# A fused attention and two-layer mixture kernel: attention units in pairs, the w_out decode on 1024 columns, and a new order of steps

## The chip, the cores and the metric

One core of a Trainium2 chip runs the whole program. The metric is the device time of one execution in microseconds (us): median of three runs. Engines are TensorE (PE, matmuls), VectorE (DVE), ScalarE (ACT), GpSimd (POOL) and SyncE (SP). Here SP issues every transfer between DRAM and on-chip memory, in one queue of instructions. "SBUF" is the on-chip memory and "PSUM" the accumulators that PE writes.

## The reference, cut to what matters

Three blocks follow each other: windowed attention, a layer with SoLU and a norm, and a mixture of four experts.

```python
scores = scale * q @ k^T                       # 2 batches, 8 heads, 576 positions, 64 wide
masks  = plain window of 32 (heads 0-3), window 32*4 with step 4 (heads 4-7)
attn   = exp(scores - max); attn /= sum + 1e-9
x      = attn @ v                              # -> 1152 tokens x 512

h      = x @ w_in                              # 512 -> 1024
solu   = h * softmax(h)
ln     = (solu - mean) / sqrt(var + 1e-6) * g_ln
x      = ln @ w_out                            # 1024 -> 512

p      = domain_probs / (sum + 1e-9)           # 4 experts
out    = sum over e of p[:, e] * (relu(x @ w1[e]) @ w2[e])
```

## The kernel before, in words

**Precision.** A product of two fp32 operands is made of three matmuls on a high and a low part (hi·hi, hi·lo, lo·hi). So each operand is split before use: a cast writes the high part (`xhi`, `wh`, `hh`), a subtraction writes the low part (`xlo`, `wl`, `hl`). The attention weights `w_in` and `w_out` arrive as 64-bit numbers and are decoded by `convert` (two ACT passes, two DVE passes and one DVE or POOL pass) ahead of the split.

**Attention.** There are twelve units: for each batch, three of the plain heads (P, t = 0 to 2, 192 positions each) and three of the dilated heads (D, t = 0 to 2). A unit is the generator `att_U`, a chain of steps: scores on PE (L275, after two matmuls that write the mask, L266), maximum (L296, DVE), subtraction (L298, DVE), exponential (L301, ACT), sum (L303, DVE), reciprocal (L305, DVE), scaling into the tile `pd` (L307, POOL or DVE), transposition (PE, L326, with a copy out of PSUM, `pt`; for the five units in `ASWAP` a DVE transposition, L312, and a trip through DRAM, `da` and back), the product with v on PE (L337), and the split into `xhi` and `xlo` (L250).

**First layer.** `H.t` (t = 0 to 8) multiplies 128 tokens by `w_in` (L367: 24 matmuls of 512 columns, in four groups by the quarter of `w_in` that they need) and applies SoLU: maximum `nmx` (L372), exponential (L374), product with the sum (L376), shift (L379 or L381). `T.t` transposes the result and splits it into `hh` and `hl`. T.0 to T.2 go through PE (L398). T.3 to T.8 go through a DVE transposition (L414, L412) and through DRAM: `dt` is written, `et` is loaded, then `hh` (L174 or L176) and `hl` (L436) are made of `et`. The two `et` tiles alternate: T.3, T.5 and T.7 use `et1`, T.4, T.6 and T.8 use `et0`. `X.c.dp` multiplies a chunk c of three tiles (384 tokens) by half of `w_out` (L449, 48 matmuls of 384 columns). Chunk 0 and chunk 1 share one pair of tiles `hh`, `hl`: what T.3 to T.5 write there must wait until X.0 has read it.

**Mixture.** `up` (L562) and `down` (L634) run over eight halves of experts, with seven products for eight in `up`.

**What sets the order.** The program is written step by step by the string `ORDER`: each word advances one generator by one step, and a `+` takes the other engine where a step has two to choose from (POOL for DVE, DVE for ACT). So `ORDER` fixes the order of instructions on each engine. `F.n` stands for n matmuls that compute nothing and keep PE busy (L86). `lP`, `lD`, `lI`, `lO`, `lvp` and `lvd` are the loads. PE writes into two pools of PSUM, `psm` (H, X) and `psa` (attention, transpositions), two tiles each.

Of the kernel before, what the change touches and what calls it, by code (L numbers as in the profile page):

```python
# [27 lines left out]
EXPB = ()  # L28
ASWAP = ("UD.0.1", "UD.1.1", "UD.2.1", "UP.1.1", "UP.2.1")

ORDER = """
F.3 lP.0.0+ UP.0.0 lI.4 VI.4+ lD.0.0 VI.4 F.1 UP.0.0+ UP.0.0 lD.1.0+ VI.4 F.1 lP.1.0+ UD.0.0 UD.1.0 UP.0.0 VI.4 lI.0 UP.0.0+ VI.4 VI.0 lP.2.0 UD.0.0 UD.0.0+
UD.0.0+ UP.1.0 UP.0.0+ VI.4+ UP.0.0+ UD.1.0 UD.1.0+ UP.1.0 F.10 lD.2.0+ UP.2.0 UD.1.0+ VI.0 UD.0.0 VI.0+ VI.0 UP.1.0+ UD.1.0 UP.1.0+ VI.4+ lI.1+ UD.1.0+ VI.0+
UD.2.0+ UD.1.0+ lI.2+ F.3 UD.0.0 UD.0.0+ VI.0 UP.1.0+ UP.2.0 lvp.0.0+ VI.1+ VI.1+ UP.1.0+ UP.2.0+ VI.0 lvd.1.0+ F.1 UP.0.0 UD.2.0 UD.2.0 UP.2.0 UP.0.0 F.4
UD.1.0 UD.0.0 F.3 VI.1+ UD.1.0 VI.2+ UP.0.0 VI.2 UD.0.0 UP.2.0+ UP.1.0+ VI.1 UP.0.0 VI.1 VI.1 VI.2 UP.0.0+ lI.3 UD.1.0+ VI.2+ UP.1.0 lvp.1.0 UD.1.0 H.0+ lvd.0.0
UP.1.0 VI.3 UP.2.0+ UD.1.0+ UP.1.0 UD.2.0 UD.0.0+ VI.1 VI.3+ VI.2 VI.3 UP.1.0 UP.1.0 lD.1.1+ UD.0.0 lO.0.0+ H.0+ UD.1.1 VI.3 VI.2 UD.2.0+ lO.0.1 misc+ UD.1.1
H.1 UD.2.0 lD.0.1+ lvd.2.0+ UP.2.0+ UD.1.1+ UD.0.0 VO.0.1 VI.2+ lvp.0.1 lP.0.1 UD.2.0 lvd.2.1 H.1 VO.0.1+ UD.2.0 UD.2.0 UD.0.1 VI.3 VO.0.1+ UD.1.1 UP.0.1 UD.0.1
VI.3 lD.2.1 lvp.2.0+ lP.2.1 UD.1.1 UP.0.1 H.0 UD.0.1+ UD.0.1 UP.0.1+ UD.0.1+ UD.0.1+ UD.2.0 VO.0.1+ VI.3+ VO.0.0 UD.2.1 VO.0.0 lP.1.1+ VO.0.1+ H.0 lO.1.1+
VO.0.0 UD.2.1+ UD.2.0 UP.0.1+ UD.2.0 UD.0.1+ H.0+ H.1 H.0+ UD.0.1+ UD.0.1 UD.2.1 VO.0.0 H.1 H.0 UD.0.1+ UD.1.1 endE+ VO.0.0+ UD.2.1+ UP.2.0 UP.2.0 UD.1.1+
UP.2.1+ lvd.0.1+ VO.0.1+ lvd.1.1 UP.2.1+ UP.0.1 UD.2.1+ UP.2.0 UP.0.1 UP.2.0 VO.1.1+ VO.0.1+ VO.1.1 H.2 H.2+ H.1+ UP.2.1+ H.0+ UP.0.1+ UD.1.1+ VO.0.0+ UP.0.1  # L40
VO.1.1+ UP.2.0 VO.0.0+ H.1+ T.0 UP.2.1 UP.0.1 T.0+ UD.1.1 UD.2.1+ lO.1.0+ H.1+ T.0 UP.0.1 VO.1.1+ VO.1.1+ H.3+ UP.2.1 lO.2.1+ H.2+ T.0+ VO.1.0+ UP.0.1 UP.0.1+
VO.1.0 UD.1.1 VO.1.1+ UP.2.1+ UP.1.1+ UD.0.1 VO.1.0+ UP.1.1+ VO.1.0 H.2+ VO.1.0+ UP.1.1 UP.2.1+ UD.0.1+ UD.0.1+ H.3+ UD.2.1+ UD.1.1 H.2 H.1+ VO.1.0 UP.1.1+ T.1+
H.3+ lO.2.0+ UD.2.1+ H.2+ UD.1.1 H.3 UD.1.1 UD.2.1+ VO.2.1+ UP.1.1 VO.1.0+ H.4+ VO.2.0 VO.1.1 UP.2.1 VO.2.0 T.1+ T.2 T.1 H.3+ UP.1.1 UP.1.1+ VO.2.0+ H.4 H.5+
lvp.1.1+ UD.2.1+ H.5+ VO.2.1+ UP.2.1 H.4 T.2 VO.2.1+ VO.2.0+ VO.2.1+ lvp.2.1+ UP.2.1 VO.2.0+ lO.3.0 VO.2.1+ H.4 T.2 VO.2.1+ UP.1.1+ T.1+ T.2 lO.3.1 UP.2.1 H.3+
VO.2.0+ H.5+ UP.1.1+ VO.3.0 UP.2.1+ VO.2.0 H.5+ VO.2.1+ UP.2.1+ UP.1.1+ H.5+ VO.3.1 VO.3.0+ UD.2.1+ VO.3.1 VO.3.0 UD.2.1 X.0.1+ X.0.0 VO.3.1+ UP.1.1+ VO.3.0+
VO.3.1 VO.3.0+ VO.3.0 VO.3.1 endA T.3+ VO.3.1 VO.3.1 T.3+ UP.1.1 VO.3.0+ H.4+ T.3+ X.0.1+ T.4 X.0.0+ H.5 X.0.0 UP.1.1 T.4+ X.0.1+ T.4 T.3+ T.5+ UD.2.1 H.6+ T.3
H.8 T.3+ T.5+ H.6+ T.5 H.6 H.6+ T.4+ H.6 T.5+ H.7+ T.6 T.4 H.8 H.8 T.5 T.4 H.8+ T.5+ H.8+ H.7 X.1.0 T.6 T.6 T.6 T.8+ H.7 T.8+ H.7 T.6+ T.8+ T.6 H.7+ T.8+ X.1.0+
T.7+ T.8+ X.1.1 X.1.1+ T.7+ T.8 T.7+ sc T.7 endH T.7+ T.7 X.1.0 XQ.0 X.1.1 X.2.0 XQ.0 XQ.0 lW.0 WP.0+ WP.0 X.2.1+ XQ.0 WP.0 WP.0 WP.0 XQ.0 XQ.0 XQ.0+ WP.0 u.0+
WP.0 endX WP.0 X.2.0+ XQ.1 WP.0+ WP.0 WP.0 XQ.0+ lV.0+ WP.0 X.2.1 XQ.0+ XQ.0+ XQ.0 WP.0+ XQ.0+ XQ.0 XQ.0 WP.0 lW.1 XQ.0+ WP.0+ u.0 u.0+ XQ.1 XQ.1 WP.0 XQ.0 u.0
u.0 WP.0 WV.0 XQ.1 u.0+ WV.0 u.0 XQ.1 u.0 u.0 XQ.1+ u.1+ u.0 WP.0 u.0+ XQ.1 u.0 XQ.1+ u.0+ u.0 u.1 u.0 u.0 u.0 XQ.1 u.0+ u.0 u.0+ WV.0 WV.0 u.1+ u.0+ WP.1+ u.0  # L50
WP.1 u.1 u.1+ XQ.1+ u.0+ lW.2 u.0+ u.1 XQ.1 WP.1 lV.1 u.1 u.1 d.0 u.1+ u.1 XQ.1+ XQ.1 d.1+ u.1+ XQ.1 u.1+ WP.1 WP.1 d.0+ d.1 d.3+ WP.1+ u.1+ WP.1 XQ.1 u.1+
WP.1+ u.1 WP.1 XQ.1+ u.1+ WP.1 d.3 d.2 u.1 WP.1 d.2 u.1 WP.1 u.1 u.1+ WP.1+ u.1 WP.1+ WP.1+ u.1 u.1+ WP.1 u.1 WP.1 WP.1+
# [3 lines left out]
def fused_kernel(ctx, tc, qkp, qkd, vp, vd, w_in, w_out, gp, w1, w2, out):  # L56
# [61 lines left out]
    pds = [ap1.tile([128, 3, 128], F32, name=f"pd{i}", tag=f"pd{i}") for i in range(3)]  # L118
    sms = [ap1.tile([128, 6, 65], F32, name=f"sm{i}", tag=f"sm{i}") for i in range(3)]
    identb = ap1.tile([128, 128], BF16, name="identb", tag="identb")  # L120
    nc.vector.tensor_copy(identb, ident)
    for sm in sms:
        nc.vector.memset(sm[:, :, 64:65], 1e-9)
# [42 lines left out]
    def pick():  # L166
        return nc.gpsimd if alt[0] != late[0] else nc.vector
# [59 lines left out]
    def load_out(j, t):  # L227
        nc.sync.dma_start(out=cvr[:, 1024 * t:1024 * t + 1024].bitcast(I64), in_=w_out[256 * j + 128 * t:256 * j + 128 * t + 128, :])

    def conv_out(j, t):  # L230
        sl = slice(512 * t, 512 * t + 512)
        a = cva[:, sl]
        yield from convert(cvr[:, 1024 * t:1024 * t + 1024], a)
# [572 lines left out]
```

## Time and profile before

| what | us |
|---|---|
| median of three runs (527.78, 528.5, 528.66) | 528.5 |
| the profiled execution, its time | 528.32 |
| its span, first to last instruction | 526.5 |
| PE busy in the span | 513.6 (98%) |
| DVE busy | 356.4 (68%) |
| ACT, POOL busy | 190.6, 186.7 |

Some 1.8 us of the profiled execution's time lie outside the span. An engine's busy time is the time in which at least one of its instructions runs; PE at 98% has 12.9 us without work in the whole span.

### The profile page before, as it was taken

To read this page: it belongs to the slowest core of one execution; us is meant where nothing else is said; L and a number is where in the kernel's file an instruction comes from. 1 tells how busy PE (TensorE), PEld (TensorE's weight loads), DVE (VectorE), ACT (ScalarE), POOL (GpSimd) and SP (SyncE) were. 2 spreads that over 40 slices of the span, in tenths; PEclk is the share of its full clock that TensorE was granted. 3 is DMA by queue.
4 is the path that set the end of the run, shared out by engine and by line. 5 is a ranking of instruction groups with operands and counts; after the bars stand their busy time and mean duration, and the time that the engine had idled before them with its cause. 6 is when DMAs were issued, how large, how long until landed. Compare 5 with 4: busy or idle time off the path is not lost.

```text
span 526.5 us, 9419 instructions
## 1 busy us (share of the span) xinstructions
PE 513.6 (98%) x3971; PEld 457.9 (87%) x3971; DVE 356.4 (68%) x474; ACT 190.6 (36%) x294; POOL 186.7 (35%) x131
## 2 busy tenths in 40 slices
PE   7789999998999999999999999999999999999997
PEld 3568889888999999998989899898989989898986
DVE  7999898484999875754775485568448655853532
ACT  3766884363153422421422233142223213312200
POOL 3334321111345632830661273047117313820300
PEclk9999999999999999999999999999999999999999
DMA  8984462546062001300400040040005002000022
GB/s 321 409 319 149 146 202 78 143 159 200 1 225 95 1 1 50 111 1 1 159 1 1 8 153 0 2 153 7 2 0 161 1 0 81 0 1 1 1 81 100
DMA packets 24490, 46.44 MB, mean 88 GB/s; under 512 B 4480, under 2 KB 9088, under 8 KB 24064
## 3 DMA queue, kind: packets, MB, share of 16 engines
q1 hardware_dynamic: 24448, 45.84, 25.4%
q8 instruction: 31, 0.51, 0.4%
q14 instruction: 11, 0.09, 0.1%
HBM read 39.34 MB, written 6.49 MB: 87 GB/s over the span
## 4 chain that ended last, share of the span: by engine, by line
PE 90%; DMA 4%; DVE 2%; ACT 1%; issue 1%; SPq 1%; ACTq 0%
PE pa L634 19%; PE pm L634 18%; PE pm L562 17%; PE pa L562 17%; PE pm L367 9%; PE pm L449 6%; DMA draw<-in_moe_w_in_dram 2%; PE pa L337 1%; DMA dt<-st 1%; DMA et<-dt 1%; PE pa L275 1%; PE pa L398 1%; SPq L151 0%; DVE hl L436 0%; ACT eva L192 0%
## 5 line engine op out<-in xcount | busy, mean ns | idle before, releaser
L575 DVE SCALAR_TENSOR_TENSOR hl<-ct,hh 128x512 fp32r<-128x512 f32 (+1 forms) x64 | 64.1, 1018 | 32.4 <-ACT hh L573 32.4
L573 ACT ACTIVATE hh<-ct 128x512 fp32r<-128x512 f32 (+1 forms) x64 | 42.2, 682 | 50.8 <-DVE ct L605 21.3
L634 PE MATMUL pa<-wl,hh 128*128 128x512 f32 (+1 forms) x148 | 57.3, 387 | 0.0
L634 PE MATMUL pa<-wh,hh 128*128 128x512 f32 (+1 forms) x148 | 57.2, 387 | 0.0
L634 PE MATMUL pa<-wh,hl 128*128 128x512 f32 (+1 forms) x148 | 57.1, 386 | 0.0
L562 PE MATMUL pm<-xoh,hl 128*128 128x256 f32 (+1 forms) x192 | 56.8, 296 | 0.0
L562 PE MATMUL pa<-xoh,hl 128*128 128x256 f32 (+1 forms) x192 | 56.8, 296 | 0.0
L562 PE MATMUL pm<-xol,hh 128*128 128x256 f32 (+1 forms) x192 | 56.8, 296 | 0.0
L562 PE MATMUL pa<-xol,hh 128*128 128x256 f32 (+1 forms) x192 | 56.8, 296 | 0.0
L562 PE MATMUL pm<-xoh,hh 128*128 128x256 f32 (+1 forms) x192 | 56.8, 296 | 0.0
L562 PE MATMUL pa<-xoh,hh 128*128 128x256 f32 (+1 forms) x192 | 56.8, 296 | 0.0
L634 PE MATMUL pm<-wl,hh 128*128 128x512 f32 (+1 forms) x144 | 55.7, 387 | 0.0
L634 PE MATMUL pm<-wh,hh 128*128 128x512 f32 (+1 forms) x144 | 55.7, 387 | 0.0
L634 PE MATMUL pm<-wh,hl 128*128 128x512 f32 (+1 forms) x144 | 55.6, 386 | 0.0
L481 POOL TENSOR_TENSOR wl<-wl,wh 128x1024 fp32r<-128x1024 f32 x7 | 16.9, 2413 | 94.7 <-ACT wh L176 94.7
L639 DVE SCALAR_TENSOR_TENSOR xf<-pm,pr,xf 128x512 f32<-128x512 f32 (+1 forms) x32 | 23.6, 738 | 31.1 <-PE pm L634 31.1
L639 DVE SCALAR_TENSOR_TENSOR xf<-pa,pr,xf 128x512 f32<-128x512 f32 (+1 forms) x32 | 23.6, 738 | 30.3 <-PE pa L634 30.3
L589 POOL TENSOR_TENSOR ct<-ct,ct 128x512 f32<-128x512 f32 (+1 forms) x16 | 24.1, 1506 | 54.3 <-ACT ct L587 54.3
L176 ACT CAST wh<-wl 128x1024 fp32r<-128x1024 f32 x16 | 16.8, 1052 | 70.3 <-PE pa L634 39.8
L481 POOL TENSOR_TENSOR hl<-sw,hh 128x512 fp32r<-128x512 f32 x20 | 29.4, 1475 | 28.2 <-ACT hh L176 28.2
L562 PEld LDWEIGHTS pm<-xoh,hh 128*128 128x128 f32 x192 | 36.4, 190 | 0.3
L562 PEld LDWEIGHTS pm<-xol,hh 128*128 128x128 f32 x192 | 36.4, 190 | 0.3
(200 smaller groups left out, 1258.5 us busy)
## 6 DMA issues: line engine op xcount, KB each, us to landing
wl<-in_moe_w_dram SPq DMA_DIRECT2D x16, 512.0 KB, 4.3
cvr<-in_moe_w_out_dram SPq DMA_DIRECT2D x8, 512.0 KB, 3.5
rw<-in_moe_w_dram SPq DMA_DIRECT2D x8, 512.0 KB, 4.9
wh<-in_moe_w_dram SPq DMA_DIRECT2D x8, 512.0 KB, 6.5
draw<-in_moe_w_in_dram SPq DMA_DIRECT2D x3, 1024.0 KB, 11.9
qkD<-in_qkd_dram SPq DMA_DIRECT2D x6, 448.0 KB, 9.9
dt<-st SPq DMA_DIRECT2D x5, 512.0 KB, 3.0
et<-dt SPq DMA_DIRECT2D x10, 256.0 KB, 4.8
```

Of the source, the lines that this page charges most:

```text
L176: nc.scalar.copy(out, in_)
L275: nc.tensor.matmul(ps[32 * g:32 * g + 32, j, 64 * m:64 * m + 64], lhsT=qt[rows, h, xq:xq + 32], rhs=kt[rows, h, xq:xq + 64], start=False, ...
L337: nc.tensor.matmul(po[64 * (g % 2):64 * (g % 2) + 64, j, o:o + 32], lhsT=vt[rows, m, g, :], rhs=pt[rows, m, g, :], start=True, stop=True)
L367: nc.tensor.matmul(pm[:, n, :], lhsT=xx[:, kk, cols], rhs=ww["in", kk][:, 512 * n:512 * n + 512], start=(n_ == 0 and i < 2), stop=(n_ == K ...
L449: nc.tensor.matmul(pm[:, dd, 0:CW], lhsT=w_, rhs=x_[:, f, :], start=(f == 0 and i == 0), stop=(f == KF - 1 and i == 2))
L481: pick().tensor_tensor(out=out, in0=a, in1=b, op=op)
L562: nc.tensor.matmul(ps[:, ff, 0:n], lhsT=a[:, kk, fc], rhs=b[:, kk, :], start=kk == 0 and m == 0, stop=kk == 1 and m == 2)
L573: nc.scalar.activation(out=hv, in_=src, func=AF.Relu)
L575: nc.vector.scalar_tensor_tensor(out=lv, in0=src, scalar=0.0, in1=hv.bitcast(F32), op0=ALU.max, op1=ALU.subtract)
L589: poolv().tensor_tensor(out=c12, in0=c21, in1=c22, op=ALU.add)
L634: nc.tensor.matmul(po[:, 0, 0:dn], lhsT=h_[:, f, cols], rhs=w_, start=(f == 0 and i == 0), stop=(f == 3 and i == 2))
L639: nc.vector.scalar_tensor_tensor(out=acc[:, t, dc], in0=po[:, 0, 0:dn], scalar=pr[:, t, e:e + 1], in1=acc[:, t, dc], op0=ALU.mult, op1=ALU ...
```

## The change

The units of attention run in pairs: two units share one chain of steps, and each DVE, ACT or POOL step of the chain works on both at once, 768 elements per partition for 384. Seven chains replace twelve: in batch 0 P0 alone, D0+D1, P1 alone and P2+D2; in batch 1 P0+P1, D0+D1 and P2+D2. The matmuls are those of before. The scaling (now L304) writes in place, so the `pd` tiles go, and two `sm` tiles stand for three. Two pairs (four units) go through DRAM for the transposition, where five units did; so PE makes 24 transpositions of attention weights for 21. `conv_out` decodes `w_out` in four steps of 1024 columns for eight of 512 (its loads stay eight). The string `ORDER` is new from end to end. The core of the diff:

```diff
-EXPB = ()
-ASWAP = ("UD.0.1", "UD.1.1", "UD.2.1", "UP.1.1", "UP.2.1")
+PB = 2
+PAIRS = (((("P", 0),), (("D", 0), ("D", 1)), (("P", 1),), (("P", 2), ("D", 2))), ((("P", 0), ("P", 1)), (("D", 0), ("D", 1)), (("P", 2), ("D", 2))))
+ASWAP = ((1, 1), (2, 1))
 ORDER = """
-F.3 lP.0.0+ UP.0.0 lI.4 VI.4+ lD.0.0 VI.4 F.1 UP.0.0+ UP.0.0 lD.1.0+ VI.4 F.1 lP.1.0+ UD.0.0 UD.1.0 UP.0.0 VI.4 lI.0 UP.0.0+ VI.4 VI.0 lP.2.0 UD.0.0 UD.0.0+
+lD.0.0 lP.0.0+ F.10 lD.1.0+ U.0.0 lP.1.0+ U.0.0+ U.1.0 U.0.0 U.1.0 lP.2.0 U.0.0 lI.0 F.3 U.0.0+ U.0.0+ U.1.0 U.2.0 U.0.0+ F.1 U.1.0+ F.3 U.0.0 U.2.0 U.2.0+
...
-    def conv_out(j, t):
-        sl = slice(512 * t, 512 * t + 512)
-        a = cva[:, sl]
-        yield from convert(cvr[:, 1024 * t:1024 * t + 1024], a)
...
+    def conv_out(j):
+        yield from convert(cvr, cva)
...
+        for t in range(2):
+            sl = slice(512 * t, 512 * t + 512)
+            hi, lo = whi["out", j][:, sl], wlo["out", j][:, sl]
...
-        pick().tensor_tensor(out=pd.rearrange("p m (j x) -> p j m x", j=2), in0=sm.rearrange("p (j m) x -> p j m x", j=2),
-                             in1=st[:, 3].rearrange("p (j m) -> p j m", j=2).unsqueeze(3).to_broadcast([128, 2, 3, 64]), op=ALU.mult)
+        pick().tensor_tensor(out=sm, in0=sm, in1=st[:, 2].rearrange("p (c j) -> p c j", j=2).unsqueeze(3).to_broadcast([128, nc_, 2, 64]), op=ALU.mult)
```

Three places show what the order moves.

The first is SP's queue, the first loads of the program. The order before (`draw_196`, `draw_358`, `draw_390`, `draw_480` are pieces of `w_in`; the last three are its second, third and fourth quarter):

```order
1 L151 DMA qkP_110<-in_qkp_dram 128x832
2 L209 DMA draw_196<-in_moe_w_in_dram 128x512
3 L151 DMA qkD_113<-in_qkd_dram 128x896
4 L151 DMA qkD_114<-in_qkd_dram 128x896
5 L151 DMA qkP_111<-in_qkp_dram 128x832
6 L212 DMA draw_196<-in_moe_w_in_dram 128x512
7 L151 DMA qkP_112<-in_qkp_dram 128x832
8 L151 DMA qkD_115<-in_qkd_dram 128x896
9 L212 DMA draw_358<-in_moe_w_in_dram 128x1024
10 L212 DMA draw_390<-in_moe_w_in_dram 128x1024
11 L159 DMA vp<-in_vp_dram 128x768
12 L154 DMA vd_117<-in_vd_dram 128x768
13 L212 DMA draw_480<-in_moe_w_in_dram 128x1024
```

And with the change (`draw_505` is the fourth quarter):

```order
1 L147 DMA qkD_113<-in_qkd_dram 128x896
2 L147 DMA qkP_110<-in_qkp_dram 128x832
3 L147 DMA qkD_114<-in_qkd_dram 128x896
4 L147 DMA qkP_111<-in_qkp_dram 128x832
5 L147 DMA qkP_112<-in_qkp_dram 128x832
6 L208 DMA draw_260<-in_moe_w_in_dram 128x512
7 L147 DMA qkD_115<-in_qkd_dram 128x896
8 L205 DMA draw_260<-in_moe_w_in_dram 128x512
9 L208 DMA draw_377<-in_moe_w_in_dram 128x1024
13 L208 DMA draw_411<-in_moe_w_in_dram 128x1024
14 L147 DMA qkP_119<-in_qkp_dram 128x832
16 L208 DMA draw_505<-in_moe_w_in_dram 128x1024
```

The queries and keys of batch 0 now stand ahead of `w_in`, and two loads of batch 1 (`qkP_119`, `qkP_120`) ahead of its last quarter.

The second is DVE, the first steps of the softmax. Before (`st` is a small tile, `sm` the scores, one number per unit):

```order
12 L296 TENSOR_REDUCE st<-pa 128x6
13 L298 TENSOR_TENSOR sm_131<-pa,st 128x6x64
14 L194 TENSOR_SCALAR cva<-cva 128x512
15 L196 SCALAR_TENSOR_TENSOR cva<-draw_196,cva 128x512
16 L303 TENSOR_REDUCE st<-sm_131 128x6
17 L198 ISA cva<-draw_196,cva 128x1024
18 L296 TENSOR_REDUCE st<-pa 128x6
19 L298 TENSOR_TENSOR sm_132<-pa,st 128x6x64
```

With the change:

```order
11 L292 TENSOR_REDUCE st<-pa 128x6
12 L294 TENSOR_TENSOR sm_128<-pa,st 128x2x3x64
13 L300 TENSOR_REDUCE st<-sm_128 128x6
14 L302 RECIPROCAL st<-st 128x6
15 L292 TENSOR_REDUCE st<-pa 128x12
16 L294 TENSOR_TENSOR sm_129<-pa,st 128x2x6x64
17 L292 TENSOR_REDUCE st<-pa 128x6
18 L294 TENSOR_TENSOR sm_128<-pa,st 128x2x3x64
19 L300 TENSOR_REDUCE st<-sm_129 128x12
```

The pair D0+D1 is one row of twelve maxima where two rows of six stood, and the decode of `w_in` (L194 to L198) no longer stands between the first softmax steps.

The third is DVE around the transpositions T.3 to T.8. Before (the number behind `et` or `st` tells tiles apart: `et_1582` is T.4's, `et_1656` T.6's; `hh` and `hl` of T.3 and T.5 are made by ACT and POOL there):

```order
141 L414 STREAM_TRANSPOSE st_1615<-e 128x8x4x32
142 L372 TENSOR_REDUCE nmx<-pm 128x1
143 L436 TENSOR_TENSOR hl<-et_1582,hh 128x8x128
144 L376 SCALAR_TENSOR_TENSOR e,nsum<-e,pm 128x1024
145 L372 TENSOR_REDUCE nmx<-pm 128x1
146 L414 STREAM_TRANSPOSE st_1659<-e 128x8x4x32
147 L376 SCALAR_TENSOR_TENSOR e,nsum<-e,pm 128x1024
148 L174 CAST hh<-et_1656 128x8x128
149 L436 TENSOR_TENSOR hl<-et_1656,hh 128x8x128
```

With the change (`et_1320` is T.3's, `et_1411` T.4's, `et_1504` T.5's and `et_1600` T.7's):

```order
114 L417 STREAM_TRANSPOSE st_1409<-e 128x8x4x32
115 L236 SCALAR_TENSOR_TENSOR wl_1415<-cva,gp_sb,wh_1414 128x512 x2
116 L170 CAST hh<-et_1320 128x8x128
117 L441 TENSOR_TENSOR hl<-et_1320,hh 128x8x128
118 L170 CAST hh<-et_1411 128x8x128
119 L419 STREAM_TRANSPOSE st_1506<-e 128x8x4x32
120 L170 CAST hh<-et_1504 128x8x128
121 L441 TENSOR_TENSOR hl<-et_1504,hh 128x8x128
122 L377 TENSOR_REDUCE nmx<-pm 128x1
123 L381 SCALAR_TENSOR_TENSOR e,nsum<-e,pm 128x1024
```

All `hh` and `hl` of chunk 1 now stand in one block, and only one `nmx` (that of H.8, row 122) comes behind it. On PE this goes with H.6 and H.7 standing ahead of X.0, so that only H.8 lies between X.0 and X.1, where H.6, H.8 and H.7 did.

## Rows read from the trace of the kernel before

**Rows 1.** The page's busy times, and windows of the core (span, busy time by engine).

```profile
PE 513.6 (98%) x3971; PEld 457.9 (87%) x3971; DVE 356.4 (68%) x474; ACT 190.6 (36%) x294; POOL 186.7 (35%) x131
...
0.00:45.00 45.00, 37.41 (x832) 25.19 (x833) 39.06 (x81) 26.51 (x42) 15.95 (x24) 1.00 0.84 320
45.00:67.00 22.00, 22.00 (x375) 18.10 (x374) 20.55 (x38) 18.10 (x32) 7.43 (x7) 1.00 0.51 159
...
100.00:147.60 47.60, 45.56 (x245) 42.70 (x244) 34.75 (x47) 16.49 (x24) 11.07 (x7) 1.00 0.38 117
147.60:526.50 378.90, 375.65 (x2221) 341.83 (x2219) 236.47 (x272) 109.02 (x166) 145.09 (x89) 1.00 0.14 48
```

**Rows 2.** Waits of PE: waiting line, releaser, us in total, times, longest.

```profile
PE pa L337 <- ACT pt L176: 1.2, 1, 1.2
PE pa L326 <- ACT pt L176: 1.1, 1, 1.1
PE pa L275 <- DMA qkD<-in_qkd_dram: 1.1, 1, 1.1
...
PE pm L449 <- DVE hl L436: 0.8, 1, 0.8
...
PE pm L449 <- POOL hl L436: 0.6, 1, 0.6
PE pm L449 <- issue: 0.6, 1, 0.6
```

**Rows 3.** SP's timeline: start, length, transfer issued.

```profile
16.42 2.85 SPq L228 DMA_DIRECT2D cvr<-in_moe_w_out_dram  x2
...
24.37 0.33 SPq L159 DMA_DIRECT2D vp<-in_vp_dram  x1
...
26.59 0.33 SPq L154 DMA_DIRECT2D vd<-in_vd_dram  x1
```

**Rows 4.** PE's timeline: start, length, instruction, idle time before in brackets.

```profile
19.53 0.84 PE L326 MATMUL pa<-ident,pd 128*128 128x128 f32 x6 [1.12 <-ACT pt L176]
...
44.70 0.49 PE L326 MATMUL pa<-ident,pd 128*128 128x128 f32 x3
...
45.94 0.90 PE L337 MATMUL pa<-pt,vp 64*64 64x32 f32 x48
46.77 0.50 PE L367 MATMUL pm<-wh,xhi 128*128 128x512 f32 x1
...
95.10 0.63 PE L367 MATMUL pm<-wh,xhi 128*128 128x512 f32 x2
...
112.44 0.44 PE L449 MATMUL pm<-hl,wh 128*128 128x384 f32 x1 [0.65 <-POOL hl L436]
```

**Rows 5.** Groups of one form up to 150 us, DVE, ACT and POOL: busy us, mean ns.

```profile
L298 DVE TENSOR_TENSOR sm<-pa,st 128x384 f32<-128x384 f32 x12 | 6.5, 552 | 0.2
...
L436 DVE TENSOR_TENSOR hl<-et,hh 128x1024 fp32r<-128x1024 f32 x4 | 4.9, 1220 | 0.1
...
L174 DVE CAST hh<-et 128x1024 fp32r<-128x1024 f32 x3 | 2.1, 692 | 5.1 <-DMA et<-dt 5.1
...
L190 ACT ACTIVATE draw<-draw 128x1024 int32<-128x1024 uint32 x3 | 3.5, 1178 | 0.3 <-DMA draw<-in_moe_w_in_dram 0.3
...
L176 ACT COPY xf<-pm 128x768 f32<-128x768 f32 x4 | 3.2, 801 | 18.0 <-PE pm L449 18.0
...
L307 POOL TENSOR_TENSOR pd<-sm,st 128x384 f32<-128x384 f32 x11 | 9.4, 859 | 21.6 <-DVE st L305 20.9 <-DVE wl L225 0.7
```

**Rows 6.** The transfers through DRAM by kind (KB each, us to landing), and one of them on ACT's timeline.

```profile
et<-dt SPq DMA_DIRECT2D x1, 512.0 KB, 3.4
...
106.05 1.05 ACT L176 CAST hh<-et 128x1024 fp32r<-128x1024 f32 x1 [2.80 <-DMA et<-dt]
```

**Rows 7.** SP's timeline at the transposition T.4: the two loads of `et0`.

```profile
97.60 1.40 SPq L431 DMA_DIRECT2D et<-dt  x2
```

**Rows 8.** DVE and POOL on the timeline at 132 us.

```profile
132.25 2.31 DVE L481 TENSOR_TENSOR xol<-xf,xoh 128x1024 fp32r<-128x1024 f32 x1
...
132.07 1.39 POOL L481 TENSOR_TENSOR sw<-rw,rw 128x512 f32<-128x512 f32 x1 [4.14 <-DMA rw<-in_moe_w_dram]
```

## What the change would do to the time: the prediction

> **What bounds the kernel now.** I read the page's busy times and the windows first [rows 1]. PE works 513.6 of 526.5 us. From 147.6 us on, in the mixture, it lacks 3.3 us in 379, and there the change leaves the order of the work much as it was. Of the other 9.6 us, 7.6 lie before 45 us and 2.0 between 100 and 147.6; between 45 and 67 us PE never waits. So two places can give or take time. The waits of PE name them [rows 2]: early it waits for copies out of PSUM (1.2 and 1.1 us), for queries and keys (1.1) and for other starts; late it waits three times ahead of the product with `w_out`, 0.8, 0.6 and 0.6 us, 2.0 in all. But PE busy does not mean PE useful: early it also runs `F` matmuls that compute nothing (26 in both orders). The early stretch is therefore judged by how far the real work has come at a given time, not by idle time. The second engine is DVE [rows 1]: 39.1 of the first 45 us and 20.6 of the next 22. A lead that PE gains early must pass that stretch.
>
> **The change, part by part.**
>
> *Pairs.* A DVE step on 384 elements takes 0.55 us [rows 5], one on 1024 (of `hl`) 1.22. On the line through both, 0.55 + 384 × 0.67/640, a step on 768 takes 0.95 us (an estimate). Two steps of 0.55 become one of 0.95. With three wide DVE steps per chain and five pairs that is 15 × 0.15 = 2.3 us of DVE; ACT, POOL and the small reciprocals gain in the same way. None of this is PE time. It counts only where PE waits for a chain, and there a pair has a price: the first unit of a pair waits for the second one's scores and for the wider step, 0.4 us at each step.
>
> *The early stretch.* I walked the first instructions of each engine by hand in the new order, with the durations of rows. The anchors are landings. Counting bytes in SP's order, the 16th load of the new order (the last quarter of `w_in`) ends at the same sum, 8672 KB, as the load whose landing released SP at 26.59 us; the ninth (the second quarter) ends at 4640 KB, where SP stood at 16.42; `qkP_120` at 7648 KB, just below the 24.37 of 7840 KB, so at 23.9 [rows 3]. From there:
> - The scores of P0 come at 5.9 us (864 KB in place of 416 lie ahead). The second quarter lands at 16.4; ACT decodes it in two passes of some 1.15 us each [rows 5] and then copies `pt` of D0+D1 (0.8 us, as the copy of 768 elements of `xf`), to 19.45. The products with v begin at 19.5.
> - The scores of batch 1's plain pair wait for `qkP_120`, 23.9 to 24.85; H.0's first quarter ends at 26.2.
> - The last quarter of `w_in` lands at 26.6. ACT decodes it in two passes and copies `pt` of P1, to 29.4, then the transpositions of P2+D2 run, the scores of D0+D1 at 30.9, H.1 from 31.9. H.0's fourth group needs POOL's low part of the last quarter, ready at 39.0, and runs from 38.85 to 40.2. H.1 ends at 43.15.
>
> Before, this point (the transposition of batch 1's first plain unit after H.1) is at 44.70, and one product with v is still to come, 0.83 us (45.94 to 46.77) [rows 4]. So the new order leads by 1.55 + 0.83 = 2.4 us. The 24 transpositions for 21 come after that point: 0.84 us for six is 0.14 each with the pipeline's fill [rows 4], taken as 0.33 for three. Left: 2.05.
>
> *45 to about 95 us.* I cost this at nothing. PE does not wait here before [rows 1]. In my walk the new order has one wait, H.4's third group for the low part of the D0+D1 pair, 0.4 us. If DVE's lead is gone, every us that DVE is late is one that PE loses (rival below).
>
> *The w_out decode.* Four steps for eight save overheads of about 1.2 us on DVE and 1.5 on ACT (the same line for 1024 against two of 512). PE is ahead of neither there. Nothing, and at most that 1.2 us if DVE should set the pace.
>
> *Two tiles moved ahead of X.0.* This is the costly part. T.3, T.4 and T.5 write the pair `hh`, `hl` that X.0 reads, so none of them may be made before X.0 ends. Before, X.0 ends at 95.10 and X.1 could begin near 111.5 (112.44 less its wait of 0.65 and the first matmul) [rows 4]: H.6, H.8 and H.7 give 16.4 us, 5.46 each. Now only H.8 does. The chain to T.5 is serial, since T.5 reuses `et1` of T.3. After X.0's end: 0.04, `hh` of T.3 0.7, `hl` 1.22 [rows 5], then SP may load `et1` again, 3.4 us for this one transfer of 512 KB [rows 6], then `hh` 0.7 and `hl` 1.22. That is 7.3 us against 5.46, and X.1's second matmul needs it: PE waits about 1.7 us. Around X.0's own start I find two shorter waits: 0.35 for `hl` of T.2 and 0.65 for the PSUM tile that H.7's product with the sum must leave (DVE has the 1024-column decode in that place). X.2 gains by the move: its last input, T.8, is transposed early enough for the 96 matmuls of X.1 to hide its trip, so the waits of 0.6 and 0.8 us ahead of it go. Late waits now 0.4 + 0.35 + 0.65 + 1.7 = 3.1 us, before 2.04. Loss 1.06.
>
> *Start of the mixture.* The loads of `w1` now stand ahead of those of `w2` on SP. By the walk the first operands keep a margin of 0.4 to 1 us. Nothing; without the margin up to 1 us.
>
> **Sum.** 528.32 − 2.4 + 0.33 + 1.06 = 527.3 us, beside a median of 528.5 for the runs shown, 0.2 above the profiled one.
>
> *A rule against it.* In one row a DVE subtraction with two SBUF operands of 1024 elements took 2.31 us while POOL ran a two-input step beside it [rows 8], against 1.22 for the usual one [rows 5]. The pairs' scalings run on POOL with two SBUF inputs (one of 384 took 0.86 before [rows 5]; one of 768 now, an estimate of 1.75). The Trainium skill, GPSIMD Engine Reference, section 1, Specifications, says that GpSimd's SBUF interfaces are shared with VectorE, with contention against DVE instructions that have two SBUF inputs; by that rule the row at 132 us is no accident, and the trace agrees in that row. What it would make of this change is a rival below.
>
> **Rivals.**
> - *The late waits do not come* (523.9 to 525.5). The order puts the decode's last parts and T.5's DRAM trip where the walk is least sure: if `hl` of T.3 or the reload of `et1` is quicker, or H.7's tile frees in time, the 3.1 us of new late waits shrink to none. 528.32 − 2.4 + 0.33 − 2.04 = 524.2. For it: PE ran without a wait from 45 to 100 us before. Against it: the serial chain after X.0 is made of four rows that do not get shorter.
> - *DVE eats the lead* (528.3 to 529.4). DVE is busy 20.6 of 22 us between 45 and 67 [rows 1]. If the pairs' wider steps come late by 2 us anywhere before X.0, PE waits there and the early lead is gone: 528.32 + 0.33, less any of the late loss that the delay takes over, 528.3.
> - *Slower: the reload of `et1` takes as long as that of `et0` did* (529.6 to 531.9). The loads of `et0` for T.4 were issued from 97.60 to 99.0 [rows 7], and ACT found them landed only at 106.05 [rows 6], 7 to 8 us in place of 3.4. If the one reload behind X.0 takes 8, PE waits 4.6 us longer: 531.9. It decides from 6.0 us on (527.3 + 2.6 = 529.9). Against it: other transfers of the same kind took 4.8 us or less (median), and nothing large is queued ahead of it.
> - *Slower: POOL beside DVE* (529 to 531). Each DVE step with two SBUF inputs that meets a POOL step costs 0.5 to 1.1 us more (2.31 − 1.22 in the one row). Three to four such meetings in the stretch where DVE sets the pace, or in the chain to T.5, cost 2 to 4 us: 527.3 + 2 to 4.
> - *No effect* (528.3): the early lead is spent waiting for `H` operands, and late waits stay as they were. It belongs to the second rival.
>
> **How the numbers follow.** A measurement of this kernel tells about 0.2% (1.06 us) from no change, so faster means below 527.4 and slower above 529.6. The forecast's case, 526.3 to 528.3, has 0.36; the late waits that do not come 0.25; the eaten lead 0.21; the slow reload 0.10; POOL beside DVE 0.08. Of the forecast's case a little over half lies below 527.4. So faster 0.20 + 0.25 + 0.02 = 0.47; slower 0.10 + 0.08 − 0.02 + 0.02 = 0.18; same 0.35. The likeliest case gives 527.3. The range reaches down into the first rival and up into the slow ones: 523.7 to 530.3, with about 0.08 left out below and 0.11 above. The likeliest case's own range is 526.3 to 528.3.
>
> **What would show it.** In the changed kernel's trace, PE should start the six transpositions of batch 1's plain pair near 43 us. Late, between H.8 and X.1 PE should wait 1 to 2.5 us, for `hl`; ahead of X.2 it should not wait. The first matmul of the mixture should come near 146.5 us for 147.6 now. The prediction is wrong if the transposition of the plain pair comes after 44.7, if PE waits over 1 us between 45 us and X.0, if the wait ahead of X.1 is under 0.5 or over 4 us, or if the mixture's own 379 us change by more than 0.5.

## The result, and the profile after

The changed kernel is slower: 534.76 us median (532.3 to 536.87, 4 runs) against 528.58 for the kernel before beside it, ratio 1.0117, 95% interval 1.0071 to 1.0163. The forecast was 527.3 with a range of 523.7 to 530.3. The profiled execution took 536.87 us, the longest of the four. The stretches below therefore add up to 8.55 us, more than the 6.2 us by which the medians differ.

The page of the changed kernel: busy times, the clock granted to PE in 40 slices, and the DMA queues (packets, MB, share of 16 engines).

```profile
PE 517.1 (97%) x3970; PEld 461.6 (86%) x3974; DVE 358.5 (67%) x437; ACT 187.0 (35%) x274; POOL 187.7 (35%) x133
...
PEclk9988999998999999999999999999999999999999
...
q8 instruction: 31, 0.51, 0.4%
```

DVE is where it was, 358.5 us for 356.4 [rows 1]. PE is busy for 3.5 us longer, with three transpositions more and otherwise the same matmuls; its clock row leaves 9 in three places, so some of them ran slower. The queue q8, "instruction", of which the prediction says nothing, carries 0.51 MB in 31 packets, as it does in the kernel before. PE has 3970 + 3974 instructions in the trace (matmuls and weight loads): about 256 to a packet.

The waits of PE in the changed kernel (waiting line, releaser, us in total, times, longest), to be held against [rows 2]:

```profile
PE pa L341 <- issue: 6.1, 2, 4.2
PE pa L341 <- ACT pt L172: 2.7, 1, 2.7
...
PE pm L454 <- DVE hh L170: 1.2, 1, 1.2
PE pm L454 <- DVE hl L441: 1.0, 2, 0.8
...
PE pm L567 <- DVE xol L486: 0.5, 1, 0.5
PE pm L372 <- DVE xlo L246: 0.3, 1, 0.3
...
PE pm L454 <- DVE e L381: 0.2, 1, 0.2
```

The largest is 6.1 us for "issue": the profile shows no releaser. The kernel before has such a wait too, in a row that [rows 2] leaves out, and its timeline has the two places (start, length, instruction, idle time before in brackets):

```profile
PE pa L337 <- issue: 1.0, 2, 0.9
...
26.90 0.36 PE L337 MATMUL pa<-pt,vp 64*64 64x32 f32 x10 [0.15 <-issue]
...
38.97 0.67 PE L337 MATMUL pa<-pt,vd 64*64 64x32 f32 x31 [0.87 <-issue]
```

PE's timeline in the changed kernel, with the two places there and, in the last line, the point for which the prediction gave 43 us:

```profile
19.19 0.90 PE L341 MATMUL pa<-pt,vp 64*64 64x32 f32 x48 [2.68 <-ACT pt L172]
19.91 1.57 PE L341 MATMUL pa<-pt,vd 64*64 64x32 f32 x95
25.66 0.21 PE L341 MATMUL pa<-pt,vd 64*64 64x32 f32 x1 [4.18 <-issue]
...
28.47 1.22 PE L372 MATMUL pm<-wh,xhi 128*128 128x512 f32 x2
...
40.91 0.73 PE L372 MATMUL pm<-wh,xhi 128*128 128x512 f32 x2
...
45.26 0.30 PE L341 MATMUL pa<-pt,vd 64*64 64x32 f32 x3 [1.87 <-issue]
45.49 1.20 PE L372 MATMUL pm<-wh,xhi 128*128 128x512 f32 x2
...
51.31 0.82 PE L323 MATMUL pa<-ident,sm 128*128 128x128 f32 x6
```

The first stop falls inside a run of 96 products with v: 95 are done, and the 96th comes 4.18 us later. It reads the same tiles, `pt` and `vd`, as the 95th, so a late tile would have held up the 95th as well. Behind each stop PE is slow: two products of 512 columns take 1.22 and 1.20 us in place of 0.73. Windows give the clock (columns as in [rows 1]; the granted clock, as a share of the full one, is the number ahead of the DMA share):

```profile
21.40:25.70 4.30, 0.12 (x8) 0.00 (x0) 3.25 (x4) 3.71 (x4) 4.30 (x4) 0.93 1.02 409
25.70:32.00 6.30, 6.30 (x111) 4.51 (x111) 3.86 (x5) 2.29 (x3) 2.81 (x2) 0.51 1.03 394
...
45.20:49.00 3.80, 3.74 (x11) 2.98 (x11) 1.88 (x3) 1.88 (x3) 0.00 (x0) 0.55 0.04 12
...
121.00:126.00 5.00, 5.00 (x23) 5.00 (x22) 3.60 (x6) 3.36 (x6) 0.00 (x0) 0.69 0.50 115
```

In the windows behind these rests of PE the granted clock is 0.51, 0.55 and 0.69: PE ran at the lower of its two levels (1.2 and 2.4 GHz) for most of each.

The late stretch of the changed kernel, in the order of PE, DVE and SP: the chain to T.5 of which the prediction spoke.

```profile
118.91 0.41 PE L454 MATMUL pm<-hh,wh 128*128 128x384 f32 x1 [1.23 <-DVE hh L170]
120.17 0.41 PE L454 MATMUL pm<-hl,wh 128*128 128x384 f32 x1 [0.85 <-DVE hl L441]
...
112.24 0.69 DVE L170 CAST hh<-et 128x1024 fp32r<-128x1024 f32 x1 [7.35 <-PE pm L454]
112.97 1.23 DVE L441 TENSOR_TENSOR hl<-et,hh 128x1024 fp32r<-128x1024 f32 x1
...
118.07 0.69 DVE L170 CAST hh<-et 128x1024 fp32r<-128x1024 f32 x1 [2.12 <-DMA et<-dt]
118.80 1.23 DVE L441 TENSOR_TENSOR hl<-et,hh 128x1024 fp32r<-128x1024 f32 x1
...
114.22 0.33 SPq L433 DMA_DIRECT2D et<-dt  x1
```

X.0 ends at 112.2 and `hl` of T.3 at 114.2. SP reloads `et1` at 114.22, its data are there at 118.07, and X.1 waits 1.23 + 0.85 us.

**Where the 8.55 us went.** The table counts the real matmuls that PE had begun by a given time, each at its spacing at full clock (0.228 us for a product of 512 columns, 0.173 for 384, 0.014 and 0.017 for scores and products with v, about 0.13 for a mask and 0.11 for a transposition, `F` at nothing). The numbers are us of work. The last column is the last but one experiment below.

| begun by (us) | before | changed | changed, two edits |
|---|---|---|---|
| 20 | 6.40 | 7.49 | 6.86 |
| 26 | 9.96 | 9.28 | 9.79 |
| 50 | 31.24 | 25.99 | 30.95 |
| 100 | 80.66 | 74.97 | 80.34 |
| 121 | 100.70 | 93.24 | 99.48 |
| 147 | 124.76 | 117.30 | 124.92 |

At 20 us the changed kernel leads by 1.1; at 50 it is 5.25 behind, at 100 5.7, at 121 7.5. Its mixture begins at 155.41 for 147.6, 7.8 later, and lasts 379.7 for 378.9 us.

The early loss differs from one execution to the next. An experiment below changes only the late stretch (a tile of its own for `et` of T.5); its profiled execution, 532.77 us, has the changed kernel's order up to 100 us. It stopped at the same two places, for 2.31 and 0.53 us, and at 50 us it had 29.6 us of work done, 1.6 less than the kernel before:

```profile
20.39 2.76 PE L341 MATMUL pa<-pt,vd 64*64 64x32 f32 x95
25.46 0.21 PE L341 MATMUL pa<-pt,vd 64*64 64x32 f32 x1 [2.31 <-issue]
```

The stop ends at nearly the same time as in the changed kernel (25.66). It is shorter because the 95 products ahead of it took 2.76 us for 1.57, at a granted clock of 0.50 from 19.4 to 25.7 us. So the places of the stops belong to the order, and their lengths, with the 5.25 us at 50 us, to this one execution.

**Theory A** of the experiments: PE's instructions come in pages of 256, one packet on q8 each, and entering one page starts the transfer of the next. While the loads of the program's start are outstanding that takes some 6 us, and an order that fills a page with short matmuls comes to its end before the next page is there. Its first support is the count at which PE stops. The windows run from the start to just ahead of a stop (PE and PEld with their counts in brackets); the first fence is the kernel before at its stops of 0.15 and 0.87 us, the second the changed one:

```profile
0.00:26.88 26.88, 20.49 (x476) 12.07 (x476) 22.59 (x53) 15.87 (x25) 8.89 (x20) 1.00 0.95 366
0.00:38.90 38.90, 31.37 (x730) 20.23 (x731) 34.23 (x73) 23.75 (x37) 13.81 (x22) 1.00 0.92 355
```

```profile
0.00:25.65 25.65, 16.04 (x474) 9.89 (x478) 19.80 (x41) 13.57 (x18) 10.77 (x24) 0.99 0.94 359
0.00:45.25 45.25, 33.70 (x855) 23.05 (x860) 34.98 (x59) 20.52 (x26) 17.56 (x28) 0.92 0.88 331
```

The sums are 952 and 1461, and 952 and 1715: the same 952 in two orders, then 509 and 763 more, which is 2 × 256 and 3 × 256 less a few (these counts leave out PE's semaphore instructions, and a trace lacks a few records). The second support is when the packets of q8 pass (us; "entered" is when PE ran the page's first instruction):

| page | entered | packet on q8 | next page begun |
|---|---|---|---|
| before, to 952 | 21.14 | 24.38 to 25.45 | 26.90 |
| before, next | 26.90 | 30.84 to 31.96 | 33.34 |
| changed, to 952 | 19.42 | 23.17 to 24.23 | 25.66 |
| changed, to 1715 | 39.56 | 42.82 to 43.83 | 45.26 |
| changed, next | 45.26 | 46.30 to 47.37 | 53.80 |

With loads outstanding a packet starts 3.2 to 3.9 us after the page is entered; in the last row, with DMA idle, after 1.0. Where PE stopped, it went on 1.4 us behind the end of the packet. A page therefore takes 5.7 to 6.4 us to get. What decides is how long PE has work in the page before it. First the changed kernel:

```profile
19.42:25.65 6.23, 2.07 (x143) 1.96 (x136) 5.23 (x7) 4.90 (x6) 5.37 (x4) 0.95 1.01 404
```

Then the kernel before:

```profile
21.14:26.88 5.74, 4.23 (x141) 3.38 (x137) 5.21 (x8) 5.74 (x10) 0.83 (x1) 1.00 1.02 399
```

The changed order has the products with v of three units in this page, 2.07 us of work. The order before has H.0's products among them: 4.23 us of work and 1.22 us of waiting for `pt`, and it stops for 0.15 us only. Without that wait for `pt` it would have come to the end of the page 1.22 us sooner and found no next page there either, by the times of the table.

The Trainium skill, Runtime: NRT & Kernel Launch, section Instruction fetch mechanics, states blocks of 256 instructions that the sequencer fetches one ahead on a queue of its own, and that the cost of crossing is mostly hidden. The trace agrees on the size, and not on the cost: 4.18 and 1.87 us were open here.

### The profile page after: what moved, and what is told of

It is laid out like the page before. It is cut to its first block, busy times and chain, and to the rows that moved or that the text cites. A ratio compares the mean times of both kernels' runs of the same rounds, so it can differ in the third digit from the quotient of the medians.

```text
span 535.1 us, 9336 instructions
## 1 busy us (share of the span) xinstructions
PE 517.1 (97%) x3970; PEld 461.6 (86%) x3974; DVE 358.5 (67%) x437; ACT 187.0 (35%) x274; POOL 187.7 (35%) x133
## 4 chain that ended last, share of the span: by engine, by line
PE 81%; DMA 6%; DVE 4%; ACT 4%; issue 3%; SPq 1%; POOL 1%; DVEq 0%; POOLq 0%; ACTq 0%
PE pa L639 19%; PE pm L639 18%; PE pm L567 16%; PE pa L567 16%; PE pm L454 6%; PE pm L372 4%; DMA et<-dt 2%; DMA draw<-in_moe_w_in_dram 2%; DMA cvr<-in_moe_w_out_dram 1%; PE pa L341 1%; ACT e L379 1%; DMA dt<-st 1%; PE pa L278 1%; SPq L147 0%; DVE e L381 0%
## 5 line engine op out<-in xcount | busy, mean ns | idle before, releaser
L486 POOL TENSOR_TENSOR hl<-sw,hh 128x512 fp32r<-128x512 f32 x22 | 32.8, 1489 | 29.6 <-ACT hh L172 24.7
```

The source lines that it names most:

```text
L486: pick().tensor_tensor(out=out, in0=a, in1=b, op=op)
```

## The experiments

Each ratio below is to runs of the kernel before on the same chip, median 528.51 to 528.80 us.

**16 more instructions ahead of the stop.** Theory A says that the place of the stop is a count.

```diff
-... VI.4 F.3 U.0.0 U.1.0 ...
+... VI.4 F.3 f.16 U.0.0 U.1.0 ...
...
+    def tiny(n=1):
+        for _ in range(n):
+            nc.tensor.matmul(warm_ps[:, 0, 0:64], lhsT=warm[:, 0:128], rhs=warm[:, 0:64], start=True, stop=True)
```

> Edit: 16 small matmuls of 64 columns that compute nothing (32 instructions of PE with their weight loads) directly ahead of the products with v of P0. Theory A (PE's instructions come in pages of 256; the page that begins near PE's 952nd instruction is fetched behind the bulk loads and lands too late): the stall named issue moves by exactly 32 instructions, so to after some 79 of the 96 products of D0+D1 where it stood after 95, it still ends between 25.0 and 25.7 us, and the time stays within 1 us of the changed kernel's (about 534). Theory B (an operand of the last product is late, for instance the widened copy or a tile of v, and the trace does not name it): the stall stays ahead of the last product of the block, whatever stands before. Theory C (the clock alone is at fault: PE rests too long and is granted 1.2 GHz): more activity ahead of the rest shortens the slow stretch, 1 to 2 us gained.

```profile
25.46 0.65 PE L348 MATMUL pa<-pt,vd 64*64 64x32 f32 x17 [2.65 <-issue]
```

The stop came 16 products earlier in the work, with 17 left of 96, and ended at 25.46 for 25.66: its place goes by the count, its end by the time since the start. An operand that came late (theory B) would have kept it ahead of the 96th product. Time 533.27 us (6 runs), ratio 1.0081 [1.0057, 1.0106], within theory A's 1 us of 534: the added matmuls fill time that is lost anyway.

**Pairs taken apart, order kept.** Every wide step of `att_U` is split in two, one per unit; the matmuls and their order stay.

```diff
-        nc.vector.tensor_reduce(out=st[:, 0].rearrange("p (j c) -> p j c", j=2), in_=sv, axis=AX.X, op=ALU.max)
+        for ui in range(nu):
+            c3, c6 = slice(3 * ui, 3 * ui + 3), slice(6 * ui, 6 * ui + 6)
+            nc.vector.tensor_reduce(out=st[:, 0].rearrange("p (j c) -> p j c", j=2)[:, :, c3], in_=sv[:, :, c3], axis=AX.X, op=ALU.max)
...
```

> Edit: the changed kernel with each wide step of a pair (maximum, subtraction, exponential, sum, scaling) issued once per unit again, 384 elements each; order, loads and every PE instruction are those of the changed kernel. Theory A: PE's stall of about 4 us after its 952nd instruction stays, and so does the time, within 1.5 us (about 533 to 536); DVE only has 2 us more work. Theory B (the loss comes from the wide steps, whose second unit makes the first one wait): 3 us or more come back, 530 to 531.

```profile
25.52 0.21 PE L351 MATMUL pa<-pt,vd 64*64 64x32 f32 x1 [3.81 <-issue]
```

535.21 us, 1.0106 [1.0068, 1.0145]. The stop stands with the 96th product as in the changed kernel. The wide steps neither cause nor cure the loss; it lies in what this run keeps, the order.

**Fewer loads outstanding.** A small transfer that reads the load two before it goes out behind each load, so that SP waits and at most some three are under way.

```diff
+    def brake(t):
+        marks.append(t)
+        if 3 <= len(marks) <= 30 and marks[-3] is not None:
+            d = dpo.tile([1, 64], F32, name=f"mk{len(marks)}", tag=f"mk{len(marks)}")
+            nc.sync.dma_start(out=d, in_=marks[-3])
```

> Edit: the changed kernel, where SP issues between the early loads small transfers that read a row of the load two or three places back, so that no more than three bulk loads are under way where eight could be. Nothing else changes. Theory A: a page of PE's instructions waits behind fewer bytes, so it is moved sooner after PE has entered the page before (3.9 us in the changed kernel), the stalls of 4.2 and 1.9 us shrink to below 2.5 and 1.0, and 2 to 5 us come back (about 529.5 to 532.5), unless the loads themselves land over 2 us later, which would take part of it. Theory B: the stall keeps its length, and the later loads make the kernel 1 to 3 us slower (536 to 538).

```profile
PE pa L354 <- ACT pt L183: 6.7, 1, 6.7
PE pa L354 <- issue: 1.9, 1, 1.9
```

The packets for the three pages in question came 3.21, 2.16 and 1.63 us after entry (3.75, 3.91 and 3.26 in the changed kernel), and the waits for issue fell from 6.1 to 1.9. But the loads themselves came later: PE waited 6.7 us for `pt`, which by itself leaves the pages more time. The time was 536.82, 1.0147 [1.0119, 1.0175], where theory A had 529.5 to 532.5, less what late loads would take. With fewer loads outstanding the packets come sooner, as the theory says; holding up the loads costs more than that gives.

The same brake in the kernel before, from its 16th load on:

> Edit: the kernel before, where from its 16th load on SP issues a load only after the one three places back has landed, as far as that one is not a raw weight. Theory A: between 26 and 40 us the pages of PE's instructions are moved sooner (3.7 to 4.3 us after PE enters a page in the kernel before), the stalls of 0.15 and 0.87 us named issue go, and 0.5 to 1.5 us are gained (527.3 to 528.3); nothing if the loads of batch 1 come too late. Rival (the pages are not what bounds the kernel before): no change, within 0.3 us, or slower by late loads.

529.47 us (10 runs), 1.0023 [0.9997, 1.0049]. Waits for issue of 0.31 and 0.43 us stayed (0.15 and 0.87 before), and the 0.5 to 1.5 us that theory A asked for were not gained.

**Without the 16 later `F` matmuls.** Fifteen of them, 30 instructions, stand ahead of the stop; without them PE is idler early, and its clock lower.

```diff
-... U.0.0 lI.0 F.3 U.0.0+ U.0.0+ U.1.0 U.2.0 U.0.0+ F.1 U.1.0+ F.3 U.0.0 U.2.0 U.2.0+
+... U.0.0 lI.0 U.0.0+ U.0.0+ U.1.0 U.2.0 U.0.0+ U.1.0+ U.0.0 U.2.0 U.2.0+
...
```

> Edit: the changed kernel without the 16 later of its 26 matmuls that compute nothing; the first ten stay. Theory A (instructions come in pages of 256, and the next page's fetch is begun only when PE enters a page, so early PE can use about 256 instructions in 6.3 us): PE has 32 instructions fewer to take in, the stall near the 958th instruction falls 32 instructions later in the program (in the scores of batch 1's plain pair), and at each page boundary up to 45 us PE is 32 instructions further, worth up to 0.8 us: 533.5 to 534.5, if the clock stays. Theory C (clock): PE rests more before 20 us, is granted 1.2 GHz earlier and longer, and 1 to 4 us are lost (536 to 538).

```profile
26.71 0.85 PE L281 MATMUL pa<-qkP 64*32 64x64 f32 x36 [2.45 <-issue]
...
0.00:26.70 26.70, 18.15 (x477) 12.01 (x478) 21.15 (x44) 13.47 (x18) 11.06 (x24) 0.74 0.95 361
...
13.00:20.00 7.00, 4.89 (x135) 3.62 (x135) 6.80 (x13) 5.08 (x8) 2.17 (x3) 0.50 1.02 409
```

531.77 us (10 runs), 1.0057 [1.0032, 1.0082]: 3 us better than the changed kernel (1.0117 [1.0071, 1.0163]; the intervals just overlap), though PE ran at half clock from 13 to 20 us. It stopped at 955, the same place within the few records that a trace lacks, now behind the products with v and 12 scores, for 2.45 us, and no other stop was longer than 0.2. A slow clock while PE waits for pages anyway cost nothing here, and the instructions left out were worth some 3 us. That is more than theory A's sum, which had 533.5 to 534.5; why is not shown. A theory that the loss comes from the clock alone falls: it had 536 to 538, the mean clock was lower (0.984 for 0.987) and the time shorter.

The same in the kernel before (23 of its 26 left out):

> Edit: the kernel before without 23 of its 26 matmuls that compute nothing; the first three stay. Theory A: 46 instructions fewer in the pages up to 39 us, so PE is up to 46 instructions further at each page's entry, worth up to 1.0 us: 527.5 to 528.5. Theory C: without them PE rests longer between 8 and 23 us, is granted 1.2 GHz and works the small matmuls and the first H at half speed: 530 to 533.

528.47 us (10 runs), 0.9997 [0.9977, 1.0017], clock 0.987. In that order the `F` matmuls buy nothing and cost nothing.

**64 short matmuls, or 11 long ones, in the kernel before.** If pages are the limit, the order before must lose too when its pages fill with short matmuls, and more than by as much PE time in long ones.

```diff
-UD.1.0 UD.0.0 F.3 VI.1+ ...
+UD.1.0 UD.0.0 F.3 f.64 VI.1+ ...
```

> The kernel before with 64 small matmuls (64 columns, 128 instructions on PE, about 2.5 us of PE time) put ahead of the first product of plain v at 20.96 us. Theory A (PE's instructions come in pages of 256, and a page needs about 6.3 us from the entry into the one before it while loads are outstanding): the page begun at 21.1 us in the kernel before begins near 22.7, the next cannot begin before 29.0, and the work ahead of it would be done near 24.6; PE stands still for about 4 us with no releaser, and the time is 4 to 6 us above the kernel before. Rival (instructions cost only their own time): 2.5 us less the wait of 1.2 for the copy behind it, 1.0 to 1.5 us, the same as the kernel with eleven long matmuls in the same place.

```diff
-UD.1.0 UD.0.0 F.3 VI.1+ ...
+UD.1.0 UD.0.0 F.14 VI.1+ ...
```

> The kernel before with 11 more matmuls of 512 columns in the same place (22 instructions on PE, about 2.4 us of PE time). Theory A: the page limit is nearer by 11 matmuls and not by 64, a stall of 0 to 1.7 us, and the time is 1.2 to 2.9 us above the kernel before, at least 2 us below the kernel with 64 small ones. Rival (own time alone): 1.0 to 1.5 us, the same as with 64 small ones.

```profile
27.85 0.80 PE L343 MATMUL pa<-pt,vd 64*64 64x32 f32 x18 [1.06 <-issue]
...
0.00:27.80 27.80, 20.10 (x474) 12.31 (x477) 20.48 (x49) 13.71 (x20) 8.06 (x19) 1.00 0.94 360
...
27.80:31.70 3.90, 3.85 (x27) 3.02 (x27) 2.60 (x6) 2.81 (x5) 0.83 (x1) 0.56 1.03 397
```

With 64 short ones PE stopped at 951 for 1.06 us, and the clock fell to 0.56 behind it; with 11 long ones it did not stop there. The times were 531.63 (5 runs; ratio 1.0056 [1.0032, 1.0079]) and 530.65 (10 runs; 1.0034 [1.0019, 1.0049]), 3.1 and 2.1 us above the kernel before. Both lie above the rival's 1.0 to 1.5. Direction and place are theory A's, its sizes are not: it had a stop of some 4 us and 4 to 6 us for the short ones; the difference between the two, 1.0 us, is half the least that it had asked for, and the two intervals overlap. The sum erred in the packet: entered at 23.02, the page's packet started at 25.27, after 2.25 us and not the 3.2 to 3.9 of the rows above.

**The late chain: a tile of its own for `et` of T.5.**

```diff
-        et = spo[0].tile([128, 4, 256], F32, name=f"et{t % 2}", tag=f"et{t % 2}")
+        et = spo[0].tile([128, 4, 256], F32, name=f"et{2 if t == 5 else t % 2}", tag=f"et{2 if t == 5 else t % 2}")
```

> Edit: T.5 gets an et tile of its own, so its load no longer waits until T.3's low part has been made of et1. The late step of the prediction (X.1 waits for the chain T.3, reload, T.5): the waits of 1.2 and 0.9 us ahead of X.1 fall below 0.7 together, the slow clock behind them (0.58 and 0.82 granted) goes, and 2.5 to 4 us come back (about 531). Rival (the chain is set by hh and hl of T.3 to T.5 on DVE and POOL after X.0's end, not by the reload): under 1 us comes back.

```profile
115.28 0.41 PE L454 MATMUL pm<-hh,wh 128*128 128x384 f32 x1 [0.43 <-DVE hh L170]
116.54 0.41 PE L454 MATMUL pm<-hl,wh 128*128 128x384 f32 x1 [0.85 <-DVE hl L441]
...
113.04 2.10 DVE L170 CAST hh<-et 128x1024 fp32r<-128x1024 f32 x1
...
112.19 2.40 POOL L441 TENSOR_TENSOR hl<-et,hh 128x1024 fp32r<-128x1024 f32 x1 [41.50 <-DMA et<-dt]
```

The reload no longer holds up X.1, and the wait fell from 2.08 to 1.28 us, not to nothing: the cast `hh` of T.5 took 2.10 us, from 113.04, while POOL's `hl` of T.4 ran from 112.19 to 114.59; alone it takes 0.69. Median 534.54, 1.0098 [1.0066, 1.0131], where some 531 was expected: no difference to the changed kernel that these runs can tell. In the profiled execution the late stretch gained: the kernel is 2.9 us behind the one before at 100 us, and its mixture begins at 151.21, 3.6 behind. So 0.7 us were lost in between, where the changed kernel lost 2.1.

**H.7 put back behind X.0.**

```diff
-... VO.2+ H.6+ H.7+ H.6 T.1 ...
+... VO.2+ H.6+ H.6 T.1 ...
...
-... X.0.0+ X.0.0 H.7+ X.0.1+ T.3+ T.3 T.4+ T.5+ T.7+ ...
+... X.0.0+ X.0.0 X.0.1+ H.7+ T.3+ T.3 T.4+ T.5+ H.7 H.7 ...
```

> Edit: the changed kernel with H.7 (its 24 matmuls and its SoLU steps) moved behind X.0 again, so that two tiles of H lie between X.0 and X.1 where one did. All before that is the changed kernel's. Late step of the prediction (X.1 waits 2.1 us for the chain T.3, T.4, T.5, and PE is then granted 0.58 and 0.82 for some 6 us, worth 1.7): both go, X.2 waits up to 1 us more for T.7 or T.8, so 2.5 to 3.8 us come back, about 531.3 at a median of 534.8. Rival (the chain moves along with the tiles and X.2 waits instead): under 1 us.

```profile
90.81 0.44 PE L457 MATMUL pm<-hh,wh 128*128 128x384 f32 x1 [3.86 <-ACT hh L175]
92.30 0.69 PE L457 MATMUL pm<-hl,wh 128*128 128x384 f32 x1 [1.06 <-DVE hl L249]
...
PE pm L375 <- ACT xf L175: 3.2, 1, 3.2
```

543.85, 1.0277 [1.024, 1.0313], where 531.3 was expected and the rival had under 1 us of change. H.7 ahead of X.0 hid the end of T.0 to T.2; without it X.0 waits 3.86 + 1.06 us. And H.8, at 119.25, waits 3.24 us more, for the copy `xf` of X.0's result out of PSUM, which ACT makes only behind H.7's exponential in this order. So the run shows what H.7 covered ahead of X.0, but by its second wait it does not show by itself what the chain to T.5 costs; neither expectation had these waits.

**Both single edits together** (no later `F`, own `et`):

> The changed kernel without its 16 later warm-up matmuls and with a tile of its own for the et of T.5: both single edits together. Theory (page supply early, serial reload late, two separate losses): 531.8 less 0.2 to 1.4, so 530.4 to 531.6, still above the kernel before by 1.7 to 2.9. Rival (one loss covers the other): 531.8 or more.

530.49 us (10 runs), 1.003 [1.0018, 1.0043], where the theory put it. This is the last column of the table above: it is within some 0.3 us of the kernel before at 50, 100 and 147 us, and 1.2 behind at 121, ahead of X.2's waits. So both losses are undone in its profiled execution (528.92). That one was the shortest of ten; why the median lies 1.6 above it stays open.

**And the cast of T.5 on ACT**, which was idle there:

```diff
-... T.3 T.4+ T.5+ T.7+ T.5+ T.7+ T.4+
+... T.3 T.4+ T.5+ T.7+ T.5 T.7+ T.4+
```

> The changed kernel without its 16 later warm-ups, with a tile of its own for the et of T.5 and with the cast hh of T.5 on ACT in place of DVE. In the kernel with only the first two edits that cast took 2.09 us on DVE beside POOL's hl of T.4 (0.70 alone), and ACT was idle for 6.4 us there. Theory (the cast is stretched by POOL beside it and its DVE turn comes late, and this holds up X.1): ACT makes hh in about 1.05 us, hl ends at least 1.3 us earlier, the waits of 0.4 and 0.8 us ahead of X.1 go, and the time is 1.0 to 2.0 us below the kernel with the two edits (530.49), 528.5 to 529.5. Rival (the transfer lands too late for that, or hl is stretched by POOL in turn): the wait stays at 0.8 us or more and the time at 530 to 530.5.

```profile
111.72 1.05 ACT L175 CAST hh<-et 128x1024 fp32r<-128x1024 f32 x1 [5.62 <-DMA et<-dt]
...
112.81 1.88 DVE L444 TENSOR_TENSOR hl<-et,hh 128x1024 fp32r<-128x1024 f32 x1 [0.68 <-ACT hh L175]
...
114.83 0.41 PE L457 MATMUL pm<-hl,wh 128*128 128x384 f32 x1 [0.79 <-DVE hl L444]
```

530.21 us (5 runs), 1.0035 [1.0021, 1.0048]: the rival's number. The transfer landed only at 111.72, and now `hl` was stretched, 1.88 us for 1.23, beside POOL (111.19 to 113.60). No version here is faster than the kernel before.

## Why the prediction was wrong

**The step that failed** is "The early stretch. I walked the first instructions of each engine by hand in the new order, with the durations of rows". The walk let PE start whatever had its operands. For operands it held: the products with v were to begin at 19.5 and began at 19.19, released by ACT's copy, as said. But PE lacked instructions, a wait that the walk did not have. The point that it put at 43.15 came at 51.31. The two stops are 6.05 us, for 0.15 + 0.87 before. The slow clock behind them costs some 4.1 more: the matmuls from 25.80 to 32.55 take 6.75 us where the same forms at full clock take 4.28, and the eight products from 45.49 to 49.02 3.53 for 1.95 (estimates from rows of the same forms). So stops and clock cost 9.1 us more than before, and at 50 us the kernel is 5.25 behind. By the difference, an estimate, the new order would have led by up to 3.9 us without them, where 2.05 was forecast; what PE would then have waited for operands is not in it, and no run shows this lead. These are the sizes of the longest execution: in the one of 532.77 us the stops were 2.84 us and the kernel 1.6 behind at 50 us. In neither is the forecast lead there. A wait for "issue", 1.0 us in two places of the kernel before, stood in its trace; the prediction did not ask what it was.

The prediction also took the transposition at 44.70 [rows 4] for batch 1's first plain unit. It belongs to P2 of batch 0; by real work done, the walked point at 43.15 answers to some 45.8 of before. The lead walked out, 2.4, stays about the same (some 2.65); the name was wrong.

The estimate for a pair's step held: the subtraction on 768 elements took 0.96 us, 0.95 forecast.

**45 to 95 us at nothing**: right in kind, but for the end of the second stop at 45.26. From 50 to 100 us 0.45 us were lost, with PE's waits of 0.3 for `xlo` and, at X.0, 0.2 for `e`, where the walk had 0.4 and, around X.0's start, 0.35 and 0.65.

**The chain to T.5**: right in kind, too small. Its transfer took 3.85 us to the first use (3.4 forecast), and PE waited 2.08 for 1.7; not counted was the clock behind that wait (0.69 in the window from 121 to 126 us: eight products take 2.56 us where they take 1.39 at full clock). From 100 us to the start of the mixture 2.1 us were lost (7.8 less 5.7) against 1.06 forecast. Ahead of X.2 PE waited 0.17 us for `hl`, where none was forecast. **The w_out decode** shows nothing, as said. **The mixture** lasts 0.8 us longer, of which PE's wait for `xol` is 0.5; the bound was 0.5.

**The rivals.** DVE did not eat the lead: between 45 us and X.0 PE waits for it 0.3 us. The slow reload did not come (3.85 us, not 8). POOL beside DVE cost nothing that shows in PE's waits in the early stretch and ahead of X.1, but took back a part of the gain as soon as the reload was out of the way (2.10 us for 0.69). In the mixture DVE's `hl` at 164.62 took 1.79 us for 0.69 beside POOL, a few steps ahead of the `xol` that PE waits 0.5 us for; whether that caused this wait is not shown. None of the rivals named the page.

## What to carry to other kernels

Where an engine that bounds the kernel shows a wait with no releaser, count its instructions up to that point in two kernels: the same count in two orders points to the supply of instructions. While large loads were outstanding here, PE did not stop where an order gave it some 6 us of work per 256 instructions. So short matmuls are to be mixed with long ones there, and filler matmuls are not always free (some 3 us in the changed kernel, nothing in the one before). A gain walked out for data is only a gain if the bounding engine could go faster at all. A rest can cost twice, since the clock may come back later. And stops of this kind differ between executions, so one profile gives their places, not their usual length.

## What the runs showed of the hardware

- PE's instructions arrive in packets of 256 (31 packets, 7,944 instructions). In the two kernels the packet for the next page starts 3.2 to 3.9 us after a page is entered at six pages between 19 and 40 us, with loads outstanding (2.25 in the run with 64 short matmuls). With DMA nearly idle, at 45 and 54 us, it starts 0.8 to 1.0 us after (1.65 once, at 38.97 in the kernel before). It then takes 0.9 to 1.1 us in the rows of the table, and 1.2 to 1.5 us more pass until an instruction of a waited-for page runs.
- After rests of 4.18, 1.87 and 2.08 us the granted clock was 0.51, 0.55 and 0.69 in the windows that follow. After the rest of 1.06 us in the run with 64 short matmuls it was 0.56. After the rest of 0.87 us that ended at 38.97 in the kernel before, the products of 512 columns ran at full clock (0.73 us for two).
- A DVE cast of 1024 elements took 0.69 us alone and 2.10 beside a POOL subtraction; a DVE subtraction 1.23 alone and 1.88. It mattered which began first: in the changed kernel the DVE subtraction that makes `wl` shared 0.64 us with a POOL step twice. It took 1.23 us where it had begun ahead of POOL (161.63, POOL from 162.22) and 1.72 where POOL had begun first (170.99, POOL from 169.87). The Trainium skill, GPSIMD Engine Reference, section 1, names contention of GpSimd with DVE instructions that have two SBUF inputs or run in a two-port mode; the rows agree on the contention. The cast with its one input is the harder hit; whether it runs in a two-port mode no run shows.
